# Attention scores by pairs of heads in float32, with folds of two tiles at once

## The chip, the core and the metric

The kernel runs on one core of a Trainium2 chip. The metric is the device time of one execution in microseconds. Before the change it is 1264.35 us, the median of three runs (1263.46 to 1269.68).

## What is computed

The reference does three things in a row, all in float32 at its borders:

```
scores = q @ k^T / 8                    # 4 batches, 8 heads, 576 rows, head dimension 64
attn   = softmax over the 32 largest scores of each row;  x = attn @ v
x      = ((x @ w_a) * (x @ w_b)) @ w_out          # 2304 tokens, 512 -> 1536 -> 512: "first MoE"
out    = gate * (relu(x @ w1[e]) @ w2[e])         # e = the token's best of 8 experts: "second MoE"
```

## The kernel before, in words

**Units, groups, tiles.** A unit is a batch and a pair of heads. There are 20: batch 0 has its four pairs twice, once for each of two groups of query rows (320 and 256 rows); the other batches have four units with both groups. A group is cut into tiles of 128 query rows. An ordinary tile ("N") has 128 rows of one head; the two heads' tiles of the same rows follow one another. A mixed tile ("M") has the last 64 rows of both heads. That makes 144 tiles: 128 N and 16 M.

**One tile** (`attn_tile`, lines 556 to 620). TensorE makes its 128x576 scores as two halves of 288 in a PSUM tile `sp` (two banks, one buffer). ScalarE copies them to SBUF as `s` (line 595). To find the 32nd largest score of a row, VectorE folds the row: `m` is the elementwise max of its halves (line 603), `n` the min (line 617). Then MAX8 gives the 8 largest of `m` (line 605), MATCH_REPLACE8 takes them out (line 613), MAX8 the next 8 (line 615), three times, and line 619 the 8 largest of `n`. GpSimd makes the negated row maximum (line 607), with which ScalarE makes the exponentials (line 610).

**A pair of tiles**. `attn_kth` (lines 628, 630) merges both lists to the threshold, for two tiles at a time. `attn_out` masks: either in one VectorE instruction (line 654), or with a compare (line 648) and a product on GpSimd (line 650), chosen by the tile's number. Then TensorE transposes the masked exponentials (line 679), ScalarE copies them, and `attn_av` multiplies by v (line 700).

**Two ways to the scores.** The first nine units (`FU`, `u.f`: 40 N tiles, 5 M tiles) keep q and k in float32 with the two heads in the upper and lower 64 partitions; a matmul uses 64 of the array's 128 rows (line 571; for M tiles line 566, 64 rows by 64 columns), and shows as two records in the trace. The other eleven units (88 N, 11 M) split q and k in two float32r parts, stacked on 128 rows (ScalarE copy, GpSimd subtraction at line 513, transposes at line 522, and a second, swapped copy of the keys `kS` by two DMAs); a tile takes four matmuls, `kT` and `kS` for each half (line 585).

**The first MoE** (`moe1`, lines 797 and 827) of a batch or group starts when its attention is done. Its matmuls are filler: they have the lowest priority on TensorE and fill the gaps between the next batch's attention. The weights are converted from float64 bits at the beginning, on ScalarE, VectorE (lines 388, 391) and GpSimd. The second MoE comes after everything.

**Order.** All instructions are recorded with a cost, a priority (`pos`, 10 per tile) and what they read and write; `Plan.emit` then simulates the engines with these costs and writes each engine's instructions in the order of that schedule. Each engine executes its own in order. A tile name has a number of buffers; the first instruction of a new tile waits for the last use of the buffer's old one. Tiles are requested by `T(pool, shape, type, name, buffers)`:

```
556    def attn_tile(i, r, j, kind, h, c, pos):
558        sp = T(p_ps, [128, 2, 512], F32, "sp", 1)
```

Of the kernel before, what the change touches and what calls it, by code (L numbers as in the profile page):

```python
# [56 lines left out]
class Plan:  # L57
    """Instructions with what they read and write; emits them in the order of a list schedule."""
# [151 lines left out]
def fused_kernel(ctx: ExitStack, tc: tile.TileContext, q, k, v, w_a, w_b, w_out, w_gate, w1, w2, out,  # L210
# [21 lines left out]
    FU = opts.get("fu", range(9))  # L232
# [45 lines left out]
    # ---------------------------------------------------------------- constants  # L278
# [27 lines left out]
    qm_t, rr_t = [], []  # L306
    for i in range(2):
        qm_t.append(cst.tile([128, 192], F32R, name=f"qm{i}"))
        nc.gpsimd.memset(fr(qm_t[i]), 0.0)
# [18 lines left out]
    QM = [P_.fixed(t) for t in qm_t]  # L328
# [6 lines left out]
    # slots that no token takes: zeros, a token id out of range  # L335
# [20 lines left out]
    def conv_bufs():  # L356
        """raw words (later the float32r parts) and float32: in buffers that the first MoE uses later"""
        i = nconv[0]
        nconv[0] += 1
        x = i % 6 if i < CB else (i - CB) % 4  # L360
        if x in (0, 1, 4, 5):
            t, n = (("gT1", HB * 256), ("gH1", HB * 256), None, None, ("gT0", HB * 320), ("gH0", HB * 320))[x]
            z = T(p_mo, [128, n], F32R, t, 1)
            return (z, lambda: fr(z()[:, 0:2 * CW])), (z, lambda: fr(z()[:, 2 * CW:3 * CW]))
        z = T(p_mo, [128, KO * 256], F32R, ("xh1", "xl1")[x - 2], 1)
        if x == 2:
            cx[0] = T(p_mo, [128, KO * 256], F32, "x21", 1)
        y, o = cx[0], (x - 2) * CW
        return (z, lambda: fr(z())), (y, lambda: y()[:, o:o + CW])
# [27 lines left out]
    def split(cost, src, hi, lo, rd, wh, wl, pos):  # L397
        """src -> float32r parts hi, lo (lo may lie over src)"""
# [28 lines left out]
    # ---------------------------------------------------------------- attention  # L427
# [3 lines left out]
    def load_unit(ui, b, p, groups, pos, after=None):  # L431
        u = Rec()
        u.b, u.p, u.f, u.first = b, p, ui in FU, ui == 0
# [9 lines left out]
        for nm, src in (("k", k), ("q", q)):  # L443
            z = T(p_at, [128, 10, 64], F32, "raw" + nm, opts.get("raw", 1))
            u.raw[nm] = z
            if u.f:
                a, e, last = u.c if nm == "q" else (0, 4, True)
                for h in range(2):
                    load(c_dma(65536 * (e - a)), pos, lambda z=z, h=h, a=a, e=e: z()[:, h + 2 * a:h + 2 * e - 1:2, :],
                         src[b, h0 + h, 0:512, :].rearrange("(p c) d -> p c d", c=4)[:, a:e], [(z, h)])  # L450
                if last:
                    load(c_dma(65536), pos, lambda z=z: z()[0:64, 8:10, :],
                         src[b, h0:h0 + 2, 512:576, :].rearrange("h s d -> s h d"), [(z, 2)])
                continue
            load(c_dma(262144), pos, lambda z=z: z()[:, 0:8, :].rearrange("p (h c) d -> p h c d", h=2),
                 src[b, h0:h0 + 2, 0:512, :].rearrange("h (p c) d -> p h c d", c=4), [(z, 0)])
            for h in range(2):
                load(c_dma(16384), pos, lambda z=z, h=h: z()[64 * h:64 * h + 64, 8, :], src[b, h0 + h, 512:576, :],
                     [(z, 1 + h)])
# [9 lines left out]
    def prep_unit(u, i, pos, step):  # L469
        u.qm, u.rr = QM[i % 2], RR[i % len(RR)]  # L470
        u.qT = T(p_at, [128, 2, 512], F32R, "qT", 2)
        u.kT = T(p_at, [128, 2, 640], F32R, "kT", 2)
        if u.f:
            u.qv, u.kv = (lambda z=z: fr(z()).rearrange("p h c -> p (h c)")[:, 0:640] for z in (u.qT, u.kT))
            for ni, (nm, z, dst) in enumerate((("k", u.kT, u.kv), ("q", u.qT, u.qv))):
                raw = u.raw[nm]
                p1 = pos + 3 * ni * step
                a, e, last = u.c if nm == "q" else (0, 4, True)
                t = T(p_ps, [128, 512], F32, "pv", 1) if u.first and nm == "q" else T(p_ps, [128, 1024], F32, "tp", 1)
                cut = [(a, e, last)] if not u.first or nm == "q" else [(0, 2, False), (2, 4, True)]  # L480
                for a, e, last in cut:
                    # with the last 64 rows behind the chunks, where both are in one piece
                    o = 128 * e if u.first and nm == "q" else 512

                    def tr(t=t, raw=raw, a=a, e=e, last=last, o=o):
                        for c in range(a, e):
                            res = nc.tensor.transpose(t()[:, c * 128:(c + 1) * 128],
                                                      raw()[:, 2 * c:2 * c + 2, :].rearrange("p a d -> p (a d)"), idf)
                        if last:
                            res = nc.tensor.transpose(t()[:, o:o + 64], raw()[0:64, 8:10, :].rearrange("p a d -> p (a d)"),  # L490
                                                      idf[0:64, 0:64])
                        return res
                    P(PE, 110 * (e - a) + 60 * last, p1, tr, r=[raw], w=[(t, a)], act=0)

                    def out(t=t, dst=dst, a=a, e=e, last=last, o=o, f=64 * (nm == "k")):
                        if last and f:
                            nc.scalar.copy(dst()[:, 0:64], t()[:, 512:S])
                        if last and 128 * e < 512:
                            nc.scalar.copy(dst()[:, 512:S], t()[:, o:o + 64])
                            last = False  # L500
                        x, y = 128 * a, S if last else 128 * e
                        return nc.scalar.copy(dst()[:, f + x:f + y], t()[:, x:y])
                    u.mark = P(ACT, c_act(128 * (e - a) + 64 * last) + (150 if last and (e < 4 or nm == "k") else 0), p1,
                               out, r=[(t, a)], w=[(z, a)])
            return
        u.kS = T(p_at, [128, 2, 640], F32R, "kS", opts.get("kS", 2))
        for ni, nm in enumerate(("k", "q")):
            raw = u.raw[nm]
            p0 = pos + 3 * ni * step
            hl = T(p_at, [128, 9, 2, 64], F32R, "hl", opts.get("hl", 1))  # L510
            P(ACT, c_act(576, True), p0, lambda raw=raw, hl=hl: nc.scalar.copy(hl()[:, :, 0, :], raw()[:, 0:9, :]),
              r=[raw], w=[(hl, 0)])
            P(POOL, c_pool(576), p0, lambda raw=raw, hl=hl: nc.gpsimd.tensor_sub(
                hl()[:, :, 1, :], raw()[:, 0:9, :], fr(hl()[:, :, 0, :])), r=[raw, (hl, 0)], w=[(hl, 1)])
            for h in range(2):
                p1 = p0 + step * (1 + h)
                t = T(p_ps, [128, 1024], F32R, "tp", 1)
                lst = [(c, 4 * h + c) for c in range(4)] + ([(4, 8)] if h else [])

                def tr(t=t, lst=lst, hl=hl):  # L520
                    for c, j in lst:
                        r = nc.tensor.transpose(t()[:, c * 128:(c + 1) * 128],
                                                hl()[:, j].rearrange("p a d -> p (a d)"), idr)
                    return r
                P(PE, 56 * len(lst), p1, tr, r=[hl], w=[t], act=0)
                if nm == "q":
                    P(ACT, c_act(512), p1, lambda t=t, h=h: nc.scalar.copy(u.qT()[:, h, :], fr(t()[:, 0:512])),
                      r=[t], w=[(u.qT, h)])
                else:
                    P(ACT, c_act(512), p1, lambda t=t, h=h: nc.scalar.copy(u.kT()[:, h, 64:576], fr(t()[:, 0:512])),  # L530
                      r=[t], w=[(u.kT, h)])
                if h and nm == "q":
                    P(ACT, 220, p1, lambda t=t: (
                        nc.scalar.copy(u.qm()[:, 0:64], fr(t()[:, 512:576])),
# [21 lines left out]
    def attn_tile(i, r, j, kind, h, c, pos):  # L556
# [41 lines left out]
        def kt(a, b):  # L598
            return r.kt()[:, j, a:b]
# [33 lines left out]
    def attn_out(i, r, j, kind, h, c, pos, s, e):  # L633
# [10 lines left out]
        def am():  # L644
            return amz()[:, o:o + S]
# [912 lines left out]
```

## Time and profile before

| | us |
|---|---|
| median of 3 runs | 1264.35 |
| the profiled execution: its span | 1266.8 |
| TensorE busy | 1150.6 |
| VectorE busy | 967.0 |
| ScalarE busy | 768.3 |
| GpSimd busy | 598.7 |

The profile is of one execution; the span runs from its first instruction to its last, and no other time of that execution is given. Engines are PE (TensorE; PEld its weight loads), DVE (VectorE), ACT (ScalarE), POOL (GpSimd), SP (SyncE, which issues DMAs). Busy time of TensorE is the union of its instructions, which overlap, as matmuls are pipelined. A view by windows gives busy times in stretches of the span; PEclk is the granted share of TensorE's full clock.

### The profile page before, as it was taken

What the parts mean: (1) busy time and instruction counts of PE and PEld (TensorE: products, weight loads), DVE (VectorE), ACT (ScalarE), POOL (GpSimd) and SP (SyncE); (2) the same over time, 40 slices, a digit from 0 to 9 for tenths busy, and PEclk for the clock granted to TensorE, in tenths of its full rate; (3) what the DMA queues carried; (4) which work ended last, traced back from release to release, by engine and by line L of the source; (5) the groups of instructions that cost most, each with busy time, mean ns of one, the idle gap of its engine ahead of it and who ended that gap; (6) DMA issues with size and microseconds to landing.
All of it is one profiled execution on the core that took longest, in us unless ns stands there. A gap on an engine that the chain in (4) does not pass through costs nothing.

```text
span 1266.8 us, 22840 instructions
## 1 busy us (share of the span) xinstructions
PE 1150.6 (91%) x7702; PEld 1002.9 (79%) x7702; DVE 967.0 (76%) x2702; ACT 768.3 (61%) x1716; POOL 598.7 (47%) x761
## 2 busy tenths in 40 slices
PE   6667779888989999999999999999899899999996
PEld 3434457666778879888878789899899889999996
DVE  7999999999999999999999999941002645444441
ACT  6667567676767777667767766643222545554451
POOL 4666668677665766525565642564423210000111
PEclk9965579897999999999999999999999999999998
DMA  7576557697746643343333523335554554554550
GB/s 228 157 240 183 147 173 231 242 319 244 242 159 231 226 159 127 123 139 119 115 116 125 169 80 125 114 110 200 182 208 155 187 179 148 185 174 149 171 178 27
DMA packets 118242, 214.89 MB, mean 170 GB/s; under 512 B 30899, under 2 KB 78515, under 8 KB 110437
## 3 DMA queue, kind: packets, MB, share of 16 engines
q1 hardware_dynamic: 114901, 203.89, 49.7%
q0 software_dynamic: 3216, 9.46, 2.0%
q8 instruction: 63, 1.03, 0.3%
q14 instruction: 62, 0.51, 0.1%
HBM read 171.82 MB, written 35.25 MB: 163 GB/s over the span
## 4 chain that ended last, share of the span: by engine, by line
DVE 46%; PE 38%; issue 8%; DMA 4%; ACT 2%; POOL 1%; SPq 1%; POOLq 0%; DVEq 0%; ACTq 0%
DVE m L613 10%; PE ab L797 10%; DVE kt L615 9%; PE ab L827 7%; DVE m L603 6%; PE ab L1155 6%; DVE n L617 4%; DVE am L654 3%; DVE am L648 3%; PE pv L1204 3%; DVE kt L605 3%; PE ms L1204 3%; DVE kt L619 3%; PE pv L700 2%; DVE kt L628 1%
## 5 line engine op out<-in xcount | busy, mean ns | idle before, releaser
L797 PE MATMUL ab<-xh,wt 128*128 128x320 f32 (+1 forms) x1344 | 309.1, 308 | 2.5 <-ACT sb L782 2.5
L797 PEld LDWEIGHTS ab<-xh,wt 128*128 128x128 f32 x1344 | 231.5, 195 | 10.2 <-issue 6.4
L797 PE MATMUL ab<-xl,wt 128*128 128x320 f32 (+1 forms) x672 | 202.3, 301 | 0.0
L613 DVE MATCH_REPLACE8 m<-kt,m 128x288 f32<-128x288 f32 x432 | 188.1, 437 | 0.0
L615 DVE MAX8 kt<-m 128x8 f32<-128x288 f32 x432 | 186.8, 443 | 0.0
L827 PE MATMUL ab<-gH,wt 128*128 128x320 f32 (+1 forms) x768 | 172.0, 304 | 3.8 <-DMA wt<-wos 3.1
L650 POOL TENSOR_TENSOR am<-am,e 128x576 f32<-128x576 f32 x78 | 123.3, 1584 | 50.7 <-DVE am L648 50.2
L827 PEld LDWEIGHTS ab<-gH,wt 128*128 128x128 f32 x768 | 130.2, 192 | 7.9 <-DMA wt<-wos 3.3
L610 ACT ACTIVATE e<-s,nm 128x576 f32<-128x576 f32 x144 | 111.8, 779 | 33.2 <-POOL nm L607 32.1
L797 PEld LDWEIGHTS ab<-xl,wt 128*128 128x128 f32 x672 | 131.0, 195 | 0.0
L1229 POOL DMA_INDIRECT out_dram<-y,ti x23 | 23.0, 1000 | 227.2 <-ACT y L1223 210.9
L805 POOL TENSOR_TENSOR sa<-sa,sb 128x320 f32<-128x320 f32 (+1 forms) x96 | 87.4, 910 | 86.0 <-ACT sb L782 85.3
L679 PE MATMUL tp<-idr,am 128*128 128x128 f32 x512 | 86.1, 302 | 40.2 <-DVE am L654 23.6
L595 ACT COPY s<-sp 128x576 f32<-128x576 f32 x144 | 91.9, 638 | 38.3 <-DVE am L654 17.4
L827 PE MATMUL ab<-gT,wt 128*128 128x320 f32 (+1 forms) x384 | 114.5, 298 | 0.0
L679 PEld LDWEIGHTS tp<-idr,am 128*128 128x128 f32 x512 | 63.2, 153 | 60.8 <-POOL am L650 22.5
L1073 DVE TENSOR_TENSOR wp<-raw,wp 128x1024 fp32r<-128x1024 f32 (+1 forms) x73 | 67.4, 942 | 54.1 <-ACT wp L1072 53.7
L603 DVE TENSOR_TENSOR m<-s 128x288 f32<-128x288 f32 x144 | 108.5, 754 | 0.0
L400 POOL TENSOR_TENSOR gT<-sa,gH 128x320 fp32r<-128x320 f32 (+1 forms) x96 | 88.0, 916 | 26.2 <-ACT gH L399 25.8
L607 POOL TENSOR_SCALAR nm<-kt 128x1 f32<-128x1 f32 x144 | 38.7, 271 | 120.7 <-DVE kt L605 97.4
L1155 PE MATMUL ab<-xgh,wp 128*128 128x304 f32 (+6 forms) x352 | 89.8, 313 | 1.6 <-DVE gT L1162 1.3
L617 DVE TENSOR_TENSOR n<-s 128x288 f32<-128x288 f32 x144 | 88.2, 612 | 0.0
(304 smaller groups left out, 2861.7 us busy)
## 6 DMA issues: line engine op xcount, KB each, us to landing
wt<-ws SPq DMA_DIRECT2D x54, 1024.0 KB, 4.9
wt<-wos SPq DMA_DIRECT2D x44, 768.0 KB, 4.5
raw<-in_moe_w_dram SPq DMA_DIRECT2D x64, 512.0 KB, 3.7
kS<-kT SPq DMA_DIRECT2D x22, 304.0 KB, 3.9
xsort<-rows SPq DMA_DIRECT2D x8, 771.0 KB, 10.4
wp<-ws SPq DMA_DIRECT2D x6, 1024.0 KB
vt<-in_v_dram SPq DMA_DIRECT2D x20, 256.0 KB, 3.2
gT<-in_moe_w_a_dram SPq DMA_DIRECT2D x8, 512.0 KB, 3.8
```

The costliest lines, as they stand in the source:

```text
L400: P(POOL, c_pool(cost), pos, lambda: nc.gpsimd.tensor_sub(lo(), src(), fr(hi())), r=rd + wh, w=wl)
L595: P(ACT, c_act(S), pos, lambda: nc.scalar.copy(s().rearrange("p (a b) -> p a b", a=2), sp()[:, :, 0:HS]), r=[sp], w=[s], label="s")
L603: P(DVE, c_dve(HS), pos, lambda: nc.vector.tensor_tensor(m(), s()[:, 0:HS], s()[:, HS:S], op=OP.max), r=[s], w=[m])
L610: P(ACT, c_act(S, True) + 90, pos, lambda: nc.scalar.activation(e(), s(), AF.Exp, bias=nm(), scale=SCALE), r=[s, nm], w=[e], label="e")
L613: P(DVE, c_dve(HS), pos, lambda x=x: nc.vector.match_replace(out=m(), in_to_replace=kt(8 * x - 8, 8 * x), in_values=m(), imm_value=NEG), r ...
L615: P(DVE, c_dve(HS), pos, lambda x=x: nc.vector.max(out=kt(8 * x, 8 * x + 8), in_=m()), r=[m], w=[KT(x)])
L617: P(DVE, c_dve(HS), pos + 0.5, lambda: nc.vector.tensor_tensor(n(), s()[:, 0:HS], s()[:, HS:S], op=OP.min), r=[s], w=[n])
L650: P(POOL, c_pool(S), pos, lambda: nc.gpsimd.tensor_mul(am(), am(), e()), r=[e], w=[amk])
L679: res = nc.tensor.transpose(tp()[:, 512 * h + x * 128:512 * h + (x + 1) * 128], z()[:, 640 * h + x * 128:640 * h + (x + 1) * 128], idf)
L797: res = nc.tensor.matmul(pa()[:, 0:n], view()[:, m, wi, ko, :], xv()[:, ko], start=(ko == 0 and x == 0), stop=(ko == KO - 1 and x == 2))
L827: res = nc.tensor.matmul(pa()[:, 0:n], wv()[:, wi, f, :], gv()[:, f, :], start=(f == 0 and x == 0), stop=(f == HB - 1 and x == 2))
L1155: res = nc.tensor.matmul(pa()[:, 0:cap], p1[ko]()[:, wi, f * 128:(f + 1) * 128], xv()[:, ko], start=(ko == 0 and i == 0), stop=(ko == KO - ...
```

## The change

All units use float32 q and k; the split, `kS`, `qm` and `FU` go. `attn_tiles` takes a list: both heads' N tiles of the same rows, or one M tile. For a pair, each half of the keys is a PSUM tile of its own that holds both heads: two matmuls, one on the upper 64 rows of the array and one on the lower, into two banks. ScalarE copies each half into `s`, now [128, 2, 576] with 3 buffers (before: [128, 576] with 6). The folds are done for both heads in one instruction, from the second half in PSUM and the first half in SBUF. `m` and `n` double in size and keep 2 and 1 buffers. The negated maximum is made once for a pair. The second head's rounds get a priority 5 later. `attn_out` reads its part of `s`.

```diff
-    def attn_tile(i, r, j, kind, h, c, pos):
+    def attn_tiles(lst, r, pos):
...
-        sp = T(p_ps, [128, 2, 512], F32, "sp", 1)
...
+        s = T(p_at, [128, 2, S], F32, "s", opts.get("s", 3))
+        m = T(p_at, [128, 2, HS], F32, "m", opts.get("m", 2))
+        n = T(p_at, [128, 2, HS], F32, "n", opts.get("n", 1))
...
+            for hf in range(2):
+                sp = T(p_ps, [128, 2, 512], F32, "sp", 1)
+
+                def score(hf=hf, sp=sp):
+                    for h in range(2):
+                        a, k0 = slice(64 * h, 64 * h + 64), 0 if h else 64
+                        res = nc.tensor.matmul(sp()[:, h, 0:HS], u.qT()[a, c * 128:(c + 1) * 128],
+                                               u.kT()[a, k0 + hf * HS:k0 + (hf + 1) * HS], start=True, stop=True)
+                    return res
+                P(PE, 510, pos, score, r=[u.qT, u.kT], w=[sp], label=f"score{u.b}")
+                P(ACT, c_act(S), pos, lambda hf=hf, sp=sp: nc.scalar.copy(
+                    s()[:, :, hf * HS:(hf + 1) * HS], sp()[:, :, 0:HS]), r=[sp], w=[(s, (h, hf)) for h in range(2)],
+                  label="s")
+        def halves(out, op):
...
+            return nc.vector.tensor_tensor(out(), sp()[:, :, 0:HS], s()[:, :, 0:HS], op=op)
+        ks = [(s, (h, 0)) for h in range(nh)]
+        for out, op in ((m, OP.max), (n, OP.min)):
+            P(DVE, c_dve(HS * nh, True), pos - 12, lambda out=out, op=op: halves(out, op), r=[sp] + ks,
+              w=[(out, h) for h in range(nh)])
...
-        P(DVE, c_dve(HS), pos, lambda: nc.vector.tensor_tensor(m(), s()[:, 0:HS], s()[:, HS:S], op=OP.max),
-          r=[s], w=[m])
...
+        nm = T(p_sml, [128, 2, 1], F32, "nm", 3)
+        P(POOL, 180, pos - 5, lambda: nc.gpsimd.tensor_scalar(
+            nm()[:, 0:nh], r.kt()[:, j0:j0 + nh, 0:1], -SCALE, None, op0=OP.mult),
+          r=[KT(j0 + h, 0) for h in range(nh)], w=[nm])
...
+            res.append((i, r, j, kind, h, c, pos + 5.0 * h, s, e))
         for x in range(1, 4):
+            for h, (i, j, kind, _, c) in enumerate(lst):
+                P(DVE, c_dve(HS), pos + 5.0 * h, lambda x=x, h=h, j=j: nc.vector.match_replace(
...
-                P(DVE, c_dve(HS), pos + 0.5, lambda: nc.vector.tensor_tensor(n(), s()[:, 0:HS], s()[:, HS:S],
-                                                                            op=OP.min), r=[s], w=[n])
...
-        pend.append(attn_tile(i, R, j, kind, h, c, pos))
+        pend.append((i, j, kind, h, c))
         if len(pend) < 2 and j < R.nt - 1:
             continue
+        made = attn_tiles(pend, R, 10.0 * pend[0][0])
         attn_kth(R, j + 1 - len(pend), j + 1, pos)
-        for x in pend:
+        for x in made:
             attn_out(*x)
```

## Rows read from the trace of the kernel before

**Rows 1.** The page's part 1: busy us (share of the span) xinstructions.
```profile
PE 1150.6 (91%) x7702; PEld 1002.9 (79%) x7702; DVE 967.0 (76%) x2702; ACT 768.3 (61%) x1716; POOL 598.7 (47%) x761
```

**Rows 2.** Busy time of every engine by windows: stretch, PE, PEld, DVE, ACT, POOL, PEclk, DMA.
```profile
0.00:165.00 165.00, 115.28 (x362) 66.92 (x362) 156.19 (x405) 112.50 (x236) 102.30 (x130) 0.74 0.64 191
165.00:270.00 105.00, 89.84 (x502) 68.51 (x501) 103.49 (x261) 73.08 (x159) 72.54 (x75) 0.90 0.73 233
270.00:440.00 170.00, 151.64 (x1079) 131.81 (x1077) 170.00 (x493) 125.81 (x304) 118.24 (x145) 0.94 0.71 233
440.00:836.00 396.00, 381.90 (x2881) 340.32 (x2880) 393.28 (x1253) 278.56 (x656) 212.81 (x292) 1.00 0.38 124
836.00:1267.00 431.00, 411.95 (x2886) 395.29 (x2884) 144.03 (x294) 178.35 (x365) 92.85 (x123) 0.98 0.48 163
```

**Rows 3.** Lines 797, 654: duration ns min/median/max, first and last start us, forms.
```profile
L797 PE MATMUL ab<-xh,wt x1344: 277/308/635, 165.6 to 910.0; 128*128 128x320 f32 x97, 128*128 128x256 f32 x95
...
L654 DVE SCALAR_TENSOR_TENSOR am<-s,kth,e x66: 792/808/1985, 34.9 to 835.5; 128x576 f32<-128x576 f32 x66
```

**Rows 4.** VectorE's largest wait, 440 to 640 us: total us, times, longest.
```profile
DVE gb L976 <- PE ms L966: 0.6, 1, 0.6
```

**Rows 5.** The folds: groups (count, busy us, mean ns), then lines (ns min/median/max).
```profile
L603 DVE TENSOR_TENSOR m<-s 128x288 f32<-128x288 f32 x144 | 108.5, 754 | 0.0
...
L617 DVE TENSOR_TENSOR n<-s 128x288 f32<-128x288 f32 x144 | 88.2, 612 | 0.0
...
L603 DVE TENSOR_TENSOR m<-s x144: 410/628/2950, 12.0 to 828.4; 128x288 f32<-128x288 f32 x144
...
L617 DVE TENSOR_TENSOR n<-s x144: 430/445/3996, 12.4 to 831.5; 128x288 f32<-128x288 f32 x144
```

**Rows 6.** Line 753, VectorE with one operand in PSUM: groups by shape, then the line.
```profile
L753 DVE TENSOR_TENSOR xf<-xc,pv 128x320 f32<-128x320 f32 x8 | 3.8, 471 | 0.1
L753 DVE TENSOR_TENSOR xf<-xc,pv 128x256 f32<-128x256 f32 x8 | 3.3, 410 | 2.8 <-PE pv L742 2.8
...
L753 DVE TENSOR_TENSOR xf<-xc,pv x16: 391/440/486, 495.5 to 847.0; 128x320 f32<-128x320 f32 x8, 128x256 f32<-128x256 f32 x8
```

**Rows 7.** Windows of line 603 alone, then 617 alone: stretch, DVE busy (count), PEclk, DMA.
```profile
0.00:165.00 165.00, 25.03 (x24) 0.74 0.64 191
165.00:270.00 105.00, 14.15 (x15) 0.90 0.73 233
...
0.00:165.00 165.00, 13.84 (x23) 0.74 0.64 191
165.00:270.00 105.00, 13.32 (x16) 0.90 0.73 233
```

**Rows 8.** TensorE's timeline at 193 us (start us, us); line 571 to its second, then fourth record.
```profile
193.42 0.31 PE L797 MATMUL ab<-xl,wt 128*128 128x320 f32 x1
193.57 0.31 PE L797 MATMUL ab<-xh,wt 128*128 128x320 f32 x1
...
193.81 0.75 PE L571 MATMUL sp<-kT,qT 64*128 64x288 f32 x2
...
193.81 1.23 PE L571 MATMUL sp<-kT,qT 64*128 64x288 f32 x4
194.97 0.41 PE L797 MATMUL ab<-xh,wt 128*128 128x320 f32 x1
```

**Rows 9.** TensorE's timeline at 530 us: first of four split score matmuls, and what follows.
```profile
530.41 0.29 PE L585 MATMUL sp<-kT,qT 128*128 128x288 f32 x1
...
530.94 0.31 PE L827 MATMUL ab<-gH,wt 128*128 128x320 f32 x1
```

**Rows 10.** TensorE's timeline at 260 us: the scores of a mixed tile.
```profile
260.48 1.19 PE L566 MATMUL sp<-kT,qT 64*64 64x288 f32 x8
```

**Rows 11.** TensorE's largest wait, 440 to 640 us: total us, times, longest.
```profile
PE tp L679 <- DVE am L654: 4.3, 4, 1.8
```

More of the change, by code (lines that the diff above doesn't have):

```diff
@@ L305, in fused_kernel @@
     nc.gpsimd.memset(wg, 0.0)
[L306 to L309, printed above, removed]
+    rr_t = []
     for i in range(opts.get("rr", 1)):
@@ L327, in fused_kernel @@
         nc.gpsimd.memset(gb_t[i], 0.0)
-    QM = [P_.fixed(t) for t in qm_t]
     RR = [P_.fixed(t) for t in rr_t]
@@ L469, in prep_unit @@
     def prep_unit(u, i, pos, step):
[L470 to L505, printed above, removed]
@@ new lines, in prep_unit, with tr, out @@
+        u.rr = RR[i % len(RR)]
+        u.qT = T(p_at, [128, 640], F32, "qT", 2)
+        u.kT = T(p_at, [128, 640], F32, "kT", 2)
+        for ni, (nm, z) in enumerate((("k", u.kT), ("q", u.qT))):
+            raw = u.raw[nm]
+            p1 = pos + 3 * ni * step
+            a, e, last = u.c if nm == "q" else (0, 4, True)
+            t = T(p_ps, [128, 512], F32, "pv", 1) if u.first and nm == "q" else T(p_ps, [128, 1024], F32, "tp", 1)
+            cut = [(a, e, last)] if not u.first or nm == "q" else [(0, 2, False), (2, 4, True)]
+            for a, e, last in cut:
+                o = 128 * e if u.first and nm == "q" else 512
+                def tr(t=t, raw=raw, a=a, e=e, last=last, o=o):
+                    for c in range(a, e):
+                        res = nc.tensor.transpose(t()[:, c * 128:(c + 1) * 128],
+                                                  raw()[:, 2 * c:2 * c + 2, :].rearrange("p a d -> p (a d)"), idf)
+                    if last:
+                        res = nc.tensor.transpose(t()[:, o:o + 64], raw()[0:64, 8:10, :].rearrange("p a d -> p (a d)"),
+                                                  idf[0:64, 0:64])
+                    return res
+                P(PE, 110 * (e - a) + 60 * last, p1, tr, r=[raw], w=[(t, a)], act=0)
+                def out(t=t, dst=z, a=a, e=e, last=last, o=o, f=64 * (nm == "k")):
+                    if last and f:
+                        nc.scalar.copy(dst()[:, 0:64], t()[:, 512:S])
+                    if last and 128 * e < 512:
+                        nc.scalar.copy(dst()[:, 512:S], t()[:, o:o + 64])
+                        last = False
+                    x, y = 128 * a, S if last else 128 * e
+                    return nc.scalar.copy(dst()[:, f + x:f + y], t()[:, x:y])
+                u.mark = P(ACT, c_act(128 * (e - a) + 64 * last) + (150 if last and (e < 4 or nm == "k") else 0), p1,
+                           out, r=[(t, a)], w=[(z, a)])
@@ L570, in score_f @@
-            for hf in range(2):
-                res = nc.tensor.matmul(sp()[:, hf, 0:HS], u.qv()[a, c * 128:(c + 1) * 128],
-                                       u.kv()[a, k0 + hf * HS:k0 + (hf + 1) * HS], start=True, stop=True)
-            return res
-        def score():
-            if kind == "M":
-                lst = [(u.qm()[:, 0:128], 0), (u.qm()[:, 64:192], 1)]
-            else:
-                lst = [(u.qT()[:, h, c * 128:(c + 1) * 128], h)]
-            n = 2 * len(lst)
-            for hf in range(2):
-                x = 0
-                for st, hh in lst:
-                    for kk in (u.kT(), u.kS()):
-                        res = nc.tensor.matmul(sp()[:, hf, 0:HS], st, kk[:, hh, k0 + hf * HS:k0 + (hf + 1) * HS],
-                                               start=(x == 0), stop=(x == n - 1))
-                        x += 1
-            return res
```

131 lines of the change are left out of this document (45 added, 86 removed).

## The prediction

> **What bounds the kernel now.** I read the page's busy shares first, then busy times by stage, then the waits of the engine that is full, then single groups and stretches of the timeline.
>
> VectorE's 967 us look like three quarters of the span and TensorE's 1151 us like nine tenths [rows 1]. Both are averages over stages. The first filler matmul (line 797) starts at 165.6 us and the attention's last mask product (line 654) at 835.5 us [rows 3]; I cut the span there. By stages [rows 2], VectorE is busy 156 of the first 165 us, 103 of the next 105, all 170 of the third stretch and 393 of 396 in the fourth; in the last 431 us it is busy for a third. TensorE has much idle time in the first stretch and 15 us in the second, then 170 - 151.6 = 18.4 us and 396 - 381.9 = 14.1 us. So there are three regimes: up to about 270 us VectorE alone sets the pace; from 270 to 836 us VectorE and TensorE are both almost full; after that TensorE is. VectorE's waits confirm it: the largest between 440 and 640 us is 0.6 us [rows 4]. What it lacks is time, not data.
>
> Inside this busy time there is waiting. The two folds of a tile (elementwise max and min of the two halves of a score row, lines 603 and 617) average 754 and 612 ns, 196.7 us in all, though the shortest take 410 and 430 and the longest 2950 and 3996 [rows 5]. The same operation with one operand in PSUM (line 753) averages 471 ns for 320 elements and 410 for 256, and its longest takes 486 [rows 6]. GpSimd works beside both. I read this as the form with two SBUF operands being held up by GpSimd, and the form with one in PSUM not.
>
> **Part 1: folds of two tiles, one half from PSUM.** The 128 ordinary tiles become 64 pairs with two folds of 2x288 elements; the 16 mixed tiles keep two folds of 288. Line 753 gives 61 ns for 64 elements more, 0.95 ns each: at that slope 576 elements take 410 + 320 x 0.95 = 715 ns, by plain proportion 471 x 576/320 = 848. I take 740, near the slope because the fixed part is paid once, and 440 ns for 288 [rows 6]. New total: 64 x 2 x 0.74 + 16 x 2 x 0.44 = 109 us. VectorE saves 197 - 109 = 88 us (74 at 848 ns). The other end: undisturbed folds of today cost 144 x (0.43 + 0.445) = 126 us [rows 5], so 71 of the 197 us are hold-up; if all of it falls on the other instructions with two SBUF operands (mask products, weight conversion), only 88 - 71 = 17 us are left. I take 88 for the folds, since the instructions that follow a fold read one tensor, and discount it by stages.
>
> In the first 270 us, 39 max folds and as many min folds cost 25.0 + 14.2 + 13.8 + 13.3 = 66.3 us [rows 7]; of the new total they take 39/144, 29.5 us. VectorE is the bound here, so up to 37 us come off the end. Its weight conversion still meets GpSimd there, so I take 30; the lower end is 39/144 of 17, 5 us.
>
> **Part 2: scores of two heads side by side.** Up to the ninth unit a tile's scores are four float32 matmul records on 64 rows, one after another. Between filler matmuls they start at 193.81 us and the next filler at 194.97; two records more add 1.23 - 0.75 = 0.48 us, so 0.24 each, and 1.16 us are four of them and 0.20 going out. Going in costs 193.81 - 193.57 = 0.24 us where one filler matmul follows another after 0.15 [rows 8]: 0.09 more. That is 1.25 us a tile, 2.5 for two. In the later eleven units a tile's four split matmuls on 128 rows take 530.94 - 530.41 = 0.53 us [rows 9], 1.06 for two tiles.
>
> After the change a pair has two stretches of four records, two at a time. That two can run at a time is seen in the mixed tile: eight 64x64 records take 1.19 us [rows 10] where four 64x128 ones take 1.23 [rows 8]. A stretch then costs 0.09 + 2 x 0.24 + 0.20 = 0.77 us, a pair 1.54. The 16 pairs of the first eight units and the 4 of the ninth gain 0.96 us each; the 44 later pairs lose 0.48 each, +21 us of TensorE, and their 11 mixed tiles, eight records for eight split matmuls, 0.2 each, +2. Bounds for the 44 pairs: without the edges 0.96 us a pair, -4 us; not side by side 2.5 us, +63 us.
>
> The Trainium skill (TensorEngine Tiling (Array Packing), Key Properties) says that changing the tiling mode drains TensorE. That speaks against this change; the page gives no figure, and the trace agrees, with 0.09 and 0.20 us. By the page's doubling alone, without a drain, the sum would have the -4 above in place of +21.
>
> Between 270 and 836 us TensorE's work grows by 21 + 2 - 4 (the ninth unit) = 19 us. Its idle time there is 18.4 + 14.1 = 32.5 us [rows 2]. VectorE frees 88 - 37 = 51 us in the same stretch, more than TensorE can follow. So TensorE becomes the bound and the stretch shortens by 32.5 - 19 = 13 us.
>
> **Part 3: preparation without the split.** For eleven units the float32r copies, GpSimd's subtractions, 18 transposes and two copies of the keys by DMA go; ten float32 transposes, eight of them in full width, and fewer ScalarE copies come. On TensorE I cost that at nothing: fewer instructions, each dearer. From 440 to 836 us ScalarE is busy 279 and GpSimd 213 of 396 us and the DMA engines 38% [rows 2]: these lie beside. The new loads of q and k write in shorter pieces, six issues as before, requested most of a unit ahead; that lead hides them, and without it each unit would stand for its loads once. SyncE's queue loses 22 issues.
>
> **Part 4: waits that are added.** Each pair's second score tile in PSUM is now held until ScalarE's copy and both folds (1.48 us) are done. The name has one buffer, so the next pair's first score waits, and behind it on TensorE all filler. TensorE's largest wait between 440 and 640 us is 4.3 us in all, for line 654's products [rows 11]; none that matters is for score buffers. A pair takes VectorE some 10 us ((836 - 270)/108 tiles x 2), its scores and copies a few, so I cost this at nothing; the price if it bites is in the rivals. On VectorE the folds wait for the second score and the copy of the first half; behind them stand the rounds of the pair before. The negated maximum is taken once for two tiles, so the first tile's exponential starts one MAX8 later; ScalarE's room covers it.
>
> **Sum.** 30 + 13 = 43 us off the profiled execution's 1266.8 us gives 1224; that span is 2.4 us above the median of the runs, 1264.35, so **1221 us**. What is late next is TensorE, from about 240 us to the end.
>
> **Rivals.**
> - TensorE has more room than its busy time shows. Weight loads are busy 131.8 + 340.3 us of the 566 between 270 and 836 us, 83%, but 395.3 of 431, 92%, in the last stretch [rows 2]. If 92% can be had, 515 us would do: 51 us of room, less 19, so 32 instead of 13, and 1202 us. The Trainium skill (Trainium Kernel Development and Optimization, Performance Expectations) says to judge by the busy share of weight loads and not by that of matmuls. Against it: the attention's transposes and mode changes are in that stretch and not in the last. Chance 0.18. At its extreme VectorE stays the bound throughout: 1264 - 88 = 1176 us, 0.04.
> - The hold-ups move to other instructions: 17 us of VectorE's 88 remain, 1247 us or a little more. For it: lines 628 and 654 have two SBUF operands too, and line 654 takes 792 to 1985 ns [rows 3]. Against: behind a fold stand one-operand instructions. 0.12.
> - Slower: the single score buffer. If TensorE reaches the next pair's score while this pair's folds are still ahead in VectorE's queue, it stands for them, up to 1.48 us a pair, and from 270 to 836 us little absorbs that: 44 x 1.48 = 65 us and 19 of mode changes, less 32 of idle time, less the early 30: 1264 + 22 = 1286 us. It decides from 43/44, about 1 us a pair. For it: one buffer, and an order written beforehand that doesn't see which engine is late. Against: VectorE will be the engine with room. 0.09.
> - Scores of full width do not run side by side, since only 64x64 tiles show it: +63 in place of +21 leaves 32.5 - 61 = -29 for the stretch, which eats the early 30: 1264 us, no change. 0.05.
>
> The forecast itself has 0.52. **Range.** 1190 to 1258: it takes in the first rival, the moved hold-ups and the early stage's 5 to 37 us, and leaves out the two last and VectorE as the bound throughout. A measurement here tells about 0.5%, 6 us. Faster (below 1258): 0.52 + 0.22 + 0.08 of the 0.12 = 0.82; same: 0.04 of it and part of the last rival, 0.07; slower: the buffer and the rest, 0.11.
>
> **What would show it.** Folds of 2x288 near 740 ns with a narrow spread; VectorE with idle time after 270 us, ended by TensorE or ScalarE; TensorE busy over 97% there; the first filler matmul near 150 us; the attention's end near 793 us and still about 431 us after it; a stretch of four score records in some 0.7 us. It is wrong if TensorE idles before scores for folds, if the mask products grow longer, or if VectorE stays full to the attention's end.

## The result and the profile after

The changed kernel takes 1246.09 us (median of 5 runs, 1243.6 to 1250.73) against 1265.78 us of the kernel before in the same rounds: ratio 0.9845, 95% interval [0.9819, 0.9871]. It is faster by 20 us; 43 were forecast. The time is inside the range, the gain is less than half of what was said. The profiled execution is the slowest of the five: 1250.73 us, span 1248.9.

The page of the changed kernel, part 1 (busy us, share of the span, instructions):

```profile
PE 1136.4 (91%) x7614; PEld 950.9 (76%) x7614; DVE 893.8 (72%) x2574; ACT 741.5 (59%) x1639; POOL 539.2 (43%) x673
```

VectorE lost 73 us of busy time [rows 1]. The chain of work that ended last (the page's part 4) was 46% VectorE and 38% TensorE before; it is now 20% and 62%. By windows, the same stretches as in [rows 2]:

```profile
0.00:165.00 165.00, 96.42 (x374) 54.95 (x375) 154.53 (x403) 115.12 (x244) 105.00 (x121) 0.75 0.64 196
165.00:270.00 105.00, 91.01 (x538) 69.50 (x538) 99.37 (x268) 77.31 (x169) 73.21 (x73) 0.86 0.78 243
270.00:440.00 170.00, 159.85 (x1114) 123.85 (x1112) 158.20 (x510) 124.86 (x297) 102.84 (x132) 0.96 0.65 217
440.00:836.00 396.00, 394.26 (x2837) 322.37 (x2836) 338.87 (x1108) 253.16 (x587) 177.65 (x243) 1.00 0.34 113
836.00:1249.00 413.00, 394.89 (x2758) 380.20 (x2757) 142.79 (x288) 171.06 (x344) 80.50 (x107) 0.98 0.49 166
```

Up to 165 us VectorE is as full as before. From 270 us it has idle time, and TensorE is busy 394.3 of 396 us. The folds of pairs (line 545; ns min/median/max, then groups with count, busy us, mean ns) answer to [rows 5]:

```profile
L545 DVE TENSOR_TENSOR m<-sp,s x64: 719/756/770, 13.0 to 798.2; 128x576 f32<-128x576 f32 x64
L545 DVE TENSOR_TENSOR n<-sp,s x64: 727/750/779, 13.6 to 798.8; 128x576 f32<-128x576 f32 x64
...
L545 DVE TENSOR_TENSOR m<-sp,s 128x576 f32<-128x576 f32 x64 | 48.2, 753 | 18.9 <-ACT s L537 17.1 <-PE sp L533 1.8
L545 DVE TENSOR_TENSOR n<-sp,s 128x576 f32<-128x576 f32 x64 | 48.1, 752 | 4.6 <-ACT s L537 4.6
```

The mixed tiles' folds (line 544) take 14.5 us more, 455 and 448 ns in the mean. All folds together take 110.8 us instead of 196.7, and none is held up: the slowest pair fold is 8% over the fastest. A stretch of scores on TensorE's timeline, for [rows 8]:

```profile
500.53 0.28 PE L758 MATMUL ab<-xh,wt 128*128 128x256 f32 x1
500.74 0.76 PE L533 MATMUL sp<-kT,qT 64*128 64x288 f32 x4
501.42 0.66 PE L640 MATMUL tp<-idr,am 128*128 128x128 f32 x4
```

The next instruction starts 0.68 us after the first of the four records (the ends on the timeline are modelled); before, it was 1.16 us for four records one after another. So two heads do run side by side at full width. From the filler's last start to the scores' first it is 0.21 us where 0.12 is usual, 0.09 more, as in [rows 8].

**Where the time went.** The end is the start of TensorE's filler, plus TensorE's busy time from there, plus its idle time from there. Two views give all three: the first start of the filler's line (797 before, 758 after), and a window from there to the end (second number: its length; third: TensorE's busy time).

The kernel before:
```profile
165.60:1266.80 1101.20, 1034.72 (x7341) 935.94 (x7340) 810.20 (x2296) 655.81 (x1480) 495.84 (x632) 0.98 0.50 167
```

The changed kernel:
```profile
L758 PE MATMUL ab<-xh,wt x1344: 274/308/633, 160.1 to 893.0; 128*128 128x320 f32 x97, 128*128 128x256 f32 x95
...
160.10:1248.90 1088.80, 1042.13 (x7253) 897.32 (x7251) 744.14 (x2183) 629.22 (x1401) 437.43 (x555) 0.97 0.49 162
```

The filler starts 165.6 - 160.1 = 5.5 us earlier; TensorE's busy time from there grows by 7.4 us; its idle time falls from 1101.2 - 1034.7 = 66.5 to 46.7, by 19.8 us. Together 17.9 us, the difference of the two spans. The table has the same three terms for every kernel below (single profiles; a few us of each are scatter). The second term holds the granted clock too, which the trace shows at 2.4 or at 1.2 GHz: from the filler's start on its mean is 0.974 of full speed in the changed kernel, 0.980 in early_masks and 0.967 in hybrid.

| kernel | ratio to before [95%] | filler starts | TensorE busy after | idle after |
|---|---|---|---|---|
| before | 1 | 165.6 | 1034.7 | 66.5 |
| changed | 0.9845 [0.9819, 0.9871] | 160.1 | 1042.1 | 46.7 |
| sbuf_folds | 0.9914 [0.9897, 0.9932] | 161.6 | 1040.4 | 55.5 |
| psum_before | 0.9937 [0.9920, 0.9954] | 169.8 | 1031.1 | 57.2 |
| dup_early | 0.9924 [0.9900, 0.9947] | 160.5 | 1039.4 | 53.3 |
| dup_late | 0.9867 [0.9851, 0.9884] | 160.6 | 1037.8 | 49.3 |
| less_pe | 0.9778 [0.9760, 0.9797] | 161.0 | 1017.4 | 58.0 |
| hybrid | 0.9820 [0.9802, 0.9837] | 160.5 | 1024.3 | 60.3 |
| no_pool_masks | 0.9767 [0.9744, 0.9790] | 148.2 | 1039.7 | 50.2 |
| early_masks | 0.9698 [0.9664, 0.9732] | 146.7 | 1031.8 | 46.1 |
| before_masks | 0.9950 [0.9931, 0.9969] | 164.6 | 1035.7 | 61.3 |
| hybrid_masks | 0.9743 [0.9710, 0.9776] | 148.5 | 1024.8 | 65.3 |
| recost | 1.0004 [0.9991, 1.0017] | 160.0 | 1041.2 | 62.1 |
| order_only | 0.9826 [0.9795, 0.9857] | 157.7 | 1036.8 | 46.7 |

### The profile page after: what moved, and what is told of

Its sections match the earlier page's. It is cut to its first block, busy times and chain, and to the rows that moved or that the text cites. A ratio compares the mean times of both kernels' runs of the same rounds, so it can differ in the third digit from the quotient of the medians.

```text
span 1248.9 us, 22260 instructions
## 1 busy us (share of the span) xinstructions
PE 1136.4 (91%) x7614; PEld 950.9 (76%) x7614; DVE 893.8 (72%) x2574; ACT 741.5 (59%) x1639; POOL 539.2 (43%) x673
## 4 chain that ended last, share of the span: by engine, by line
PE 62%; DVE 20%; issue 7%; DMA 5%; ACT 3%; POOL 2%; SPq 1%; POOLq 0%; ACTq 0%; DVEq 0%
PE ab L758 20%; PE ab L788 11%; PE sp L533 5%; PE ab L1116 5%; DVE m L569 4%; PE pv L661 4%; DVE kt L572 4%; PE tp L640 3%; PE ms L1165 3%; PE pv L1165 3%; DVE am L609 2%; DVE kt L556 1%; DMA xsort<-rows,pi 1%; DVE am L615 1%; DVE m L545 1%
## 5 line engine op out<-in xcount | busy, mean ns | idle before, releaser
L758 PEld LDWEIGHTS ab<-xh,wt 128*128 128x128 f32 x1344 | 228.3, 192 | 30.3 <-issue 22.6
L569 DVE MATCH_REPLACE8 m<-kt,m 128x288 f32<-128x288 f32 x432 | 190.6, 447 | 0.0
L533 PE MATMUL sp<-kT,qT 64*128 64x288 f32 x512 | 111.2, 514 | 40.5 <-ACT s L537 13.0
L766 POOL TENSOR_TENSOR sa<-sa,sb 128x320 f32<-128x320 f32 (+1 forms) x96 | 80.2, 836 | 149.2 <-ACT sb L743 145.6
L788 PEld LDWEIGHTS ab<-gH,wt 128*128 128x128 f32 x768 | 129.8, 193 | 14.9 <-issue 10.1
L611 POOL TENSOR_TENSOR am<-am,e 128x576 f32<-128x576 f32 x78 | 119.1, 1532 | 31.8 <-DVE am L609 25.7
L640 PE MATMUL tp<-idr,am 128*128 128x128 f32 x512 | 87.9, 307 | 24.7 <-DVE am L615 12.3
L537 ACT COPY s<-sp 128x576 f32<-128x576 f32 x128 | 81.8, 639 | 41.9 <-PE sp L533 31.0
L395 POOL TENSOR_TENSOR gT<-sa,gH 128x320 fp32r<-128x320 f32 (+1 forms) x96 | 82.6, 861 | 39.5 <-ACT gH L394 38.1
L640 PEld LDWEIGHTS tp<-idr,am 128*128 128x128 f32 x512 | 65.7, 157 | 44.4 <-POOL am L611 14.4
L533 PEld LDWEIGHTS sp<-kT,qT 64*128 64x128 f32 x512 | 44.1, 209 | 72.3 <-issue 28.2
L644 ACT COPY aT<-tp 128x512 f32<-128x512 f32 x128 | 73.4, 586 | 24.6 <-PE tp L640 23.7
```

The costliest lines, as they stand in the source:

```text
L395: P(POOL, c_pool(cost), pos, lambda: nc.gpsimd.tensor_sub(lo(), src(), fr(hi())), r=rd + wh, w=wl)
L533: res = nc.tensor.matmul(sp()[:, h, 0:HS], u.qT()[a, c * 128:(c + 1) * 128], u.kT()[a, k0 + hf * HS:k0 + (hf + 1) * HS], start=True, stop= ...
L537: P(ACT, c_act(S), pos, lambda hf=hf, sp=sp: nc.scalar.copy(s()[:, :, hf * HS:(hf + 1) * HS], sp()[:, :, 0:HS]), r=[sp], w=[(s, (h, hf)) f ...
L569: P(DVE, c_dve(HS), pos + 5.0 * h, lambda x=x, h=h, j=j: nc.vector.match_replace(out=m()[:, h], in_to_replace=kt(j, 8 * x - 8, 8 * x), in_ ...
L611: P(POOL, c_pool(S), pos, lambda: nc.gpsimd.tensor_mul(am(), am(), e()), r=[e], w=[amk])
L640: res = nc.tensor.transpose(tp()[:, 512 * h + x * 128:512 * h + (x + 1) * 128], z()[:, 640 * h + x * 128:640 * h + (x + 1) * 128], idf)
```

## The experiments

### Which engine paces which stage: dup_early, dup_late, less_pe

**dup_early** and **dup_late** make the min fold twice, in batch 0 (`i0 < 36`) or in batches 2 and 3 (`i0 >= 72`):

```diff
+            if op == OP.min and i0 < 36:
+                P(DVE, 1, pos - 12, lambda out=out, op=op: halves(out, op), r=[sp] + ks,
+                  w=[(out, h) for h in range(nh)])
```

> The changed kernel with the min fold made twice for the tiles of batch 0 (16 pairs and 4 mixed tiles; result unchanged): about 16 x 0.75 + 4 x 0.45 = 14 us more of VectorE before 260 us. Theory (VectorE paces only the first quarter, TensorE everything after it): most of it reaches the end, 7 to 14 us slower than the changed kernel's 1246. Rival (VectorE no longer sets the pace anywhere): under 4 us. Rival (the early stage is set by DMA or by the weight conversion): under 4 us too, and then VectorE shows idle time before 270 us filled up.

> The changed kernel with the min fold made twice for the tiles of batches 2 and 3 (32 pairs and 8 mixed tiles; result unchanged): 32 x 0.75 + 8 x 0.45 = 28 us more of VectorE between about 440 and 810 us. Theory (TensorE is the bound there): 0 to 4 us slower than 1246, VectorE's idle time there shrinks by some 28 us. Rival (VectorE still paces, its idle time is only latency that no work can use): 20 to 28 us slower.

Measured: the early copy of the fold costs 0.9924 - 0.9845, some 10 us of its 14; the late one 0.0022, under 3 us of its 28. So VectorE's work counts in the first batch and hardly in the last two. Both ends came out as the theory said, but the early one not by the filler's start: by the table it is 160.5 us against 160.1, although 14 more folds lie before it, and it is TensorE's idle time that grows, by 6.6 us.

**less_pe** takes 26 us of filler out:

```diff
-                            for x, (wi, xv) in enumerate(((0, xh), (0, xl), (1, xh))):
+                            for x, (wi, xv) in [y for y in enumerate(((0, xh), (0, xl), (1, xh))) if b != 2 or y[0] != 1]:
```

> The changed kernel without the product of the weights' high parts with the activations' low parts in the first layer of the first MoE, for batch 2 alone (that part of the sum is left out): 96 matmuls of 320 and 96 of 256 columns, 96 x 0.147 + 96 x 0.120 = 26 us less TensorE work, all filler between about 600 and 850 us. Theory (TensorE is the bound): 22 to 27 us faster than 1246. Rival (waits between the engines pace that stage): under 12 us faster, with TensorE's waits grown.

Measured: 0.9778, only 0.0067 or 8 us under the changed kernel. The theory fell here, and the rival held. TensorE is busy 25 us less and idle 11 us more. The stretch from 640 to 800 us, in the changed kernel:

```profile
640.00:800.00 160.00, 158.44 (x1135) 127.22 (x1135) 143.83 (x477) 102.64 (x237) 65.47 (x95) 1.00 0.31 108
```

and in less_pe:

```profile
640.00:800.00 160.00, 149.03 (x1031) 113.05 (x1028) 150.78 (x499) 105.51 (x247) 70.81 (x101) 1.00 0.33 113
```

TensorE now waits (149 of 160), and VectorE is busy 150.8. I read this as TensorE being the bound of that stage by only some 10 us, with VectorE and the hand-overs between them close behind; what ends the new waits was not tried.

### One part alone: sbuf_folds, psum_before, hybrid

**sbuf_folds** keeps pairs and side-by-side scores and folds from SBUF:

```diff
-            return nc.vector.tensor_tensor(out(), sp()[:, :, 0:HS], s()[:, :, 0:HS], op=op)
+            return nc.vector.tensor_tensor(out(), s()[:, :, HS:S], s()[:, :, 0:HS], op=op)
```

> The changed kernel with the folds reading both halves from SBUF (pairs and side-by-side scores stay; the score buffer is free after ScalarE's copy). Theory (the second SBUF operand is what GpSimd holds up): 2x288 folds over 1000 ns in the mean, the longest over 2500; 8 to 17 us slower than 1246, all of it lost before 270 us, and less hold-up in the weight conversion and the mask compares than in the changed kernel. Rival (pairing alone brought the gain): folds near 760 ns, within 3 us of 1246. Rival (holding the score buffer for the folds costs more than the hold-ups): faster than 1246.

```profile
L545 DVE TENSOR_TENSOR m<-s x64: 728/745/1839, 13.3 to 802.0; 128x576 f32<-128x576 f32 x64
L545 DVE TENSOR_TENSOR n<-s x64: 727/782/1952, 13.9 to 803.0; 128x576 f32<-128x576 f32 x64
```

Measured: 0.9914, some 9 us slower than the changed kernel, as expected, with smaller hold-ups than expected: the longest folds take 1839 and 1952 ns, the means are 843 and 973. The shortest are the same as from PSUM, so what the PSUM operand saves is hold-up alone. By the table the loss is mostly TensorE's idle time (55.5 against 46.7), and not the filler's start; that part of the expectation was wrong. So was the one on the mask compares, which average 652 ns here and 648 in the changed kernel.

**psum_before** is the kernel before with the folds alone from PSUM:

```diff
+        for out, op in ((m, OP.max), (n, OP.min)):
+            P(DVE, c_dve(HS, True), pos - 6, lambda out=out, op=op: nc.vector.tensor_tensor(
+                out(), sp()[:, 1, 0:HS], s()[:, 0:HS], op=op), r=[sp, s], w=[out])
```

> The kernel before, with one part of the change alone: each tile's two folds read the second half of the scores from PSUM (n with two buffers); no pairs, no side-by-side scores, split scores as before. Theory (end = the filler's start + TensorE's work from there + TensorE's idle time from there; the folds from PSUM shorten the first and the third, the side-by-side scores lengthen the second by about 8 us): folds near 450 ns with a narrow spread, ratio to before 0.977 to 0.985, as fast as the changed kernel or a little faster. Rival (the gain needs pairs and cheaper scores): ratio over 0.990. Rival (holding the score buffer for the folds costs as much as they save): ratio over 0.995, TensorE waits for line 603.

Measured: 0.9937. Its folds are as planned (445 and 442 ns in the mean), but the filler starts later than in any other kernel, at 169.8 us. This run shows most plainly where the early gain goes. The weight conversion on VectorE (lines 388 and 391) in the first 145 us, each line alone (VectorE's busy time and count, granted clock, DMA):

```profile
0.00:145.00 145.00, 19.82 (x20) 0.77 0.66 199
...
0.00:145.00 145.00, 21.43 (x19) 0.77 0.66 199
```

That is 41.3 us for 39 instructions; the kernel before took 30.3 for 38 (its lines stand under early_masks). The folds gave up 15.4 us in the same stretch (41 of them take 17.5 us, 42 took 32.9), and the conversion took 10.9 of them. Before 170 us TensorE also waits 16.9 us for folds to free the score buffer, and from 270 to 640 us VectorE waits 18.1 us for ScalarE's copies.

So the first rival holds: PSUM folds alone give 0.6%, pairs with side-by-side scores alone (sbuf_folds) 0.9%, both 1.55%; nearly a sum, with intervals of 0.2 to 0.3% to either side.

**hybrid** is the changed kernel with the split scores of before in the later eleven units:

```diff
+                        for x, kk in enumerate((u.kT(), u.kS())):
+                            res = nc.tensor.matmul(sp()[:, h, 0:HS], u.qT()[:, h, c * 128:(c + 1) * 128],
+                                                   kk[:, h, k0 + hf * HS:k0 + (hf + 1) * HS], start=(x == 0), stop=(x == 1))
```

> The changed kernel with the split scores of before (128 rows, no change of tiling mode) for the later eleven units: pairs, both heads in one score tile and folds from PSUM stay. 44 pairs x (1.55 - 1.06) = 21 us less TensorE work after 270 us. Theory (TensorE is the bound there with VectorE some 10% behind; the 26 us taken out before gave 12): 6 to 12 us faster than the changed kernel, ratio to before 0.975 to 0.980. Rival (the subtractions of the split, back on GpSimd, and ScalarE's copies undo it): ratio 0.984 or more.

Measured: 0.9820, 3 us under the changed kernel: less than the theory said, and not the rival either. TensorE's busy time is 17.8 us less, where 21 were worked out, but 13.6 us come back as idle time. A part is the clock: it is 0.937 to 0.942 over the span in the four runs, and 0.944 to 0.949 in the changed kernel's five. By the means from the filler's start, 0.967 against 0.974, I estimate some 7 us of full speed. So what the dearer late scores cost at the same clock isn't shown.

### Who holds VectorE up, and where the hold-ups went: the mask products

**no_pool_masks**, and the same edit in the kernel before, **before_masks**:

```diff
-        return any(a <= i < b and i % m < n for a, b, n, m in opts.get("mk", ((0, 72, 3, 4), (72, 144, 1, 3))))
+        return any(a <= i < b and i % m < n for a, b, n, m in opts.get("mk", ()))
```

> The changed kernel with all mask products on VectorE (78 compares of 515 to 650 ns become products of about 815 to 980) and none on GpSimd. Theory (hold-ups by GpSimd moved from the folds to the weight conversion and the masks, most of them from the conversion's own GpSimd work): in the first 146 us the conversion's instructions fall by less than a quarter of their hold-up; VectorE gets 78 x 0.3 = 23 us more work, 12 of it before 270 us; 0 to 8 us slower than the changed kernel, ratio 0.985 to 0.991. Rival (it is the mask products that hold VectorE up): conversion near its shortest times, 5 us or more faster, ratio under 0.981.

Measured: 0.9767, 10 us faster: the rival was right. VectorE's busy time is 895.5 us against 893.8 although 23 us of work were added. I had blamed the weight conversion's own GpSimd work; taking the mask products away ends most of the hold-up. The trace is less simple about which GpSimd instruction a held one meets. Before the filler's start of the changed kernel, 21 of 43 conversion instructions on VectorE take over 0.15 us longer than the 0.41 and 0.67 us of their undisturbed form, 16.8 us in all; 15 of them overlap the conversion's GpSimd work and no mask product, 4 a mask product alone, 2 both. Without the products 8 are left, with 3.1 us. I read from this that some of the effect lies in when GpSimd's conversion work falls; how much was not tried.

**early_masks** moves those of batch 0 alone, `((36, 72, 3, 4), (72, 144, 1, 3))`.

> The changed kernel with the mask products of batch 0 alone (tiles 0 to 35, 27 products) on VectorE; later tiles as in the changed kernel. Theory (GpSimd's long mask products hold the weight conversion up before the filler can start; later VectorE is not the bound): the filler starts near 148 us instead of 160, all of the gain of the run without any GpSimd products is there, ratio to before 0.974 to 0.980. Rival (that gain came from the later tiles' products and copies): filler near 148 to 155 but ratio over 0.982.

Measured: 0.9698, the fastest kernel here, 1228.8 us against the 1266.8 of the kernel before in the same rounds. That is faster than the expected range; the place of the gain, the filler's start, was right. The filler starts 13.4 us earlier than in the changed kernel. The profiled span is 24.3 us shorter; most of the rest, 10.3 us, is TensorE's busy time, with the same 7253 instructions, and some 7 us of that I estimate to be the clock (0.980 against 0.974 from the filler's start on). The conversion in the first 145 us (windows of one line alone: VectorE's busy time and count, granted clock, DMA), lines 388 and 391 of the kernel before:

```profile
0.00:145.00 145.00, 12.00 (x19) 0.75 0.65 196
...
0.00:145.00 145.00, 18.33 (x19) 0.75 0.65 196
```

The same two (now lines 383 and 386) in the changed kernel:

```profile
0.00:145.00 145.00, 18.10 (x22) 0.75 0.65 198
...
0.00:145.00 145.00, 22.24 (x21) 0.75 0.65 198
```

and in early_masks:

```profile
0.00:145.00 145.00, 11.56 (x21) 0.72 0.71 209
...
0.00:145.00 145.00, 14.60 (x21) 0.72 0.71 209
```

The change made an instruction of line 388 longer, 632 to 823 ns, and one of line 391, 965 to 1059. Without the early mask products they take 550 and 695. In this stretch 38 conversion instructions took 30.3 us before, 43 of them 40.3 after and 42 of them 26.2 without those products.

Counted up to the filler's start instead, VectorE has nearly the same conversion and mask instructions in every kernel, so their times can be laid side by side (windows of one line alone, summed; us and count):

| kernel | filler starts | folds | conversion | mask compares and products |
|---|---|---|---|---|
| before | 165.6 | 38.9 (47) | 33.1 (42) | 14.6 |
| psum_before | 169.8 | 20.9 (48) | 48.8 (46) | 15.2 |
| sbuf_folds | 161.6 | 25.6 (28) | 36.9 (42) | 19.2 |
| changed | 160.1 | 17.9 (28) | 40.3 (43) | 18.9 |
| dup_early | 160.5 | 26.8 (42) | 38.3 (42) | 14.8 |
| early_masks | 146.7 | 18.0 (28) | 26.2 (42) | 21.7 |
| before_masks | 164.6 | 39.4 (46) | 27.8 (42) | 20.8 |

This is where the folds' gain went: of the 21.0 us that they gave up, the conversion took 7.2 and the masks 4.3. In early_masks the conversion gives back 14.1. GpSimd's own part of the conversion takes about the same in both (57.9 and 56.8 us), so it is VectorE's hold-ups that end. In dup_early the 14 more folds cost 8.9 us and the others fall by 6.1: I read this as hold-up that turns up less when VectorE comes later, so that the added folds were in part free.

> The kernel before with all mask products on VectorE and none on GpSimd; folds from SBUF, tile by tile, as they were. 78 x 0.3 = 23 us more VectorE work. Theory (the folds were held up by GpSimd's mask products above all, so most of the 71 us of hold-up goes without any PSUM operand): folds under 560 ns in the mean (754 and 612 before), filler's start 8 us or more earlier, ratio 0.985 to 0.995. Rival (the hold-ups come from GpSimd's other work, so VectorE only gets longer): folds over 620 ns, ratio over 1.0.

Measured: 0.9950, on the border of what was expected. Line 603 averages 665 ns and 617 553, between theory and rival; the filler starts 1 us earlier, not 8. In the first 145 us line 603 did not get shorter at all, while lines 388 and 391 did (10.84 us for 19 and 13.30 us for 18). Line 603 there:

```profile
0.00:145.00 145.00, 22.93 (x20) 0.67 0.66 196
```

That is 1147 ns each; before, 25.0/24 = 1043 up to 165 us [rows 7]. What GpSimd still does before the filler's start is mostly the conversion, 55 of its 75 busy us. So taking one party out of the early stage is not enough: without the products the filler starts 1.0 us earlier, with the change alone 5.5, with both 18.9.

**hybrid_masks** has both edits that had made it faster:

> The changed kernel with all mask products on VectorE and the split scores of before for the later eleven units: both edits that made it faster. Theory (the end is the filler's start plus TensorE's work and idle time from there; work taken out of TensorE late comes back as idle time because VectorE and the hand-overs are close behind): filler near 148 us, TensorE's work some 18 us less than with the masks alone, idle time up by 12 to 18, ratio 0.972 to 0.977. Rival (both gains add and more, with GpSimd free): ratio under 0.968.

Measured: 0.9743, in the range of the theory. Against no_pool_masks TensorE is busy 14.9 us less and idle 15.1 us more. Here too the clock is lower, 0.968 against 0.978 from the filler's start on.

### Does the written order matter: recost, order_only

```diff
-    return k * (max(n, 256) / 2.4 + 2.5)
+    return k * (max(n, 256) / 2.4 + 13)
...
-                P(PE, 510, pos, score, r=[u.qT, u.kT], w=[sp], label=f"score{u.b}")
+                P(PE, 770, pos, score, r=[u.qT, u.kT], w=[sp], label=f"score{u.b}")
```

> The changed kernel with the planner told TensorE's real costs (13 ns instead of 2.5 beside a split matmul's columns, 770 ns instead of 510 for a stretch of two scores): the same instructions in another written order. Theory (work, not order, sets the end): within 4 us of the changed kernel, ratio 0.981 to 0.988. Rival (the order made for wrong costs loses the gain): 8 us or more faster, ratio under 0.978.

Measured: 1.0004, all of the gain lost. Neither theory nor rival. The filler's start and TensorE's busy time are those of the changed kernel; idle time grows by 15.4 us.

**order_only** sets only 510 to 600.

> The changed kernel with one planner cost changed, a stretch of two scores at 600 ns instead of 510: the same instructions in a slightly other written order. It tells how far an end moves by order alone, which the differences of a few us between the other kernels have to be held against. Theory (order counts through TensorE's idle time): filler's start and TensorE's work within 2 us of the changed kernel's 160 and 1042, idle time and end within 6 us, ratio 0.981 to 0.989. Rival (the late stage is fragile, any new order loses what the other one lost): ratio over 0.993.

Measured: 0.9826, as expected; the filler's start and TensorE's work moved a little more than the 2 us said, to 157.7 and 1036.8. A slight change of the order moves the end by a few us, so the 3 us of hybrid can't be told from an order's luck; a large one can cost the whole gain. Which of recost's moves does it was not tried. By the traces less_pe alone keeps the order of VectorE's and ScalarE's instructions. The other edits change it, so differences of some 10 us between ends (dup_early, sbuf_folds, no_pool_masks) are not proof by themselves, nor are the 20 us of the change. The durations of single lines and the filler's start carry the argument on the early stage.

## Why the prediction was right and wrong, point by point

- **Price of the folds: right.** 740 and 440 ns were taken, 752 and 451 measured; 86 us of VectorE went, 88 were forecast. The reading that an operand in PSUM ends the folds' hold-ups is shown by sbuf_folds. The Trainium skill (SBUF — State Buffer, Who interferes with whom) says that a VectorE instruction with two SBUF inputs contends with a GpSimd instruction that reads SBUF; the trace agrees, with 1952 ns for the longest fold from SBUF and 779 from PSUM.
- **Price of the scores: right.** 0.77 us a stretch with its entry were taken; 0.68 and 0.09 measured. Side by side holds at full width.
- **The late term: right in kind, its size in part by luck.** 13 us were forecast for 270 to 836 us, as TensorE's idle time less its added work; 19.8 - 7.4 = 12.4 were measured from the filler's start to the end. Both parts came out smaller than said: the idle time of that stretch fell from 32.5 to 10.2 + 1.7 = 11.9 us and not to nothing, and 7.4 stands against 19, though it also holds the cheaper scores of the first nine units after the filler's start.
- **The early term: wrong, and this is the step that failed.** "Its weight conversion still meets GpSimd there, so I take 30": the filler's start got 5.5 us. First, the discount of 7 of 37 us was far too small. Before the filler's start the folds gave up 21.0 us; 11.5 of them went to the conversion and the masks. psum_before shows the move with the folds' change alone, and early_masks that the hold-ups go when the early mask products go. Some of the lengthening comes with pairing already (36.9 us in sbuf_folds, with folds from SBUF). Second, VectorE's gain was counted up to 270 us, but from the filler's start at 160 us TensorE has work that is only moved, not saved. Its idle time from there to 270 us did not fall (15.2 us before, 16.8 after), so in this change only the filler's start counts for the early term. The prediction's own lower end for the term was 5 us.
- **The rivals.** The moved hold-ups (0.12, 1247 us) were what happened in the early stage. Over the whole span they were not: VectorE kept 73 of the 88 us, not 17, so that the time came out at 1246 is luck for that rival. They were argued away with "behind a fold stand one-operand instructions", which is true of the tile's own chain and not of the conversion that lies between. The single score buffer does not bite late: TensorE's largest wait from 440 to 836 us is 0.6 us (first line). Earlier, the sign that the prediction named is there: TensorE waits 22.7 us in all for folds before scores, 15.7 of them before 165 us (second line: the larger group). What that costs the end was not tried by itself; sbuf_folds, which frees the buffer sooner, is slower. That weight loads show more room was wrong. The Trainium skill (Trainium Kernel Development and Optimization, Performance Expectations) says to judge by their busy share; the trace does not bear that out here, with 322.4 of 396 us, 81%, in a stretch where TensorE hardly waits.

```profile
PE ms L959 <- ACT rows L962: 0.6, 1, 0.6
...
PE sp L533 <- DVE n L544: 8.6, 3, 5.0
```

- **Still open.** TensorE keeps 46 us and more of idle time in every kernel. In the changed one 17 us of it lie between the filler's start and 270 us and 18 after 836 us, where the kernel before has 15 and 19. Why work taken out of TensorE late comes back as idle time was narrowed to VectorE's closeness in one stretch (less_pe) and to the order (recost), and not settled.

## What to carry to other kernels

When an engine is full of hold-ups, ask which other instructions meet the same partner before the hold-up is booked as saved: it goes to the next in line, unless the partner's work goes too (here the filler started 13.4 us earlier once GpSimd's early mask products went too). Look for such a move in the instructions before the point that the gain has to reach. Write the end as the start of the bound engine's work plus its work plus its idle time, and count a gain once, in one of these three. Where two engines are within a tenth of each other, expect much of the work taken from one to come back as idle time: here 11.3 of 24.7 us (less_pe) and 13.6 of 17.8 (hybrid).

## What the runs showed of the hardware that was not expected

A fold of 2x288 elements takes 719 ns at best with one operand in PSUM and 728 with both in SBUF: undisturbed, the place of the operand costs nothing. A VectorE instruction with a single tensor operand (line 388 before, 383 after) is also held up: 550 ns in the mean without GpSimd's early mask products and 823 with them. And no fold of the changed kernel overlaps a copy of scores by ScalarE: over 64 pairs the nearest starts 32 ns after a copy's end, though the program orders the folds only behind the copy of the first half; VectorE's waits for the copies sum to 21.7 us. They are waits on a semaphore, so it is an order that was built in, and no run shows what the two would do without it.
